# A decode block's tail in four quadrants of 112 columns instead of three of 128 and a doubled 64

## The chip, the cores and the metric

The kernel runs on one core of one Trainium2 chip. The metric is device time in microseconds (us) of one execution; lower is better. Three runs of the kernel before gave 213.26, 213.30 and 213.38 us.

## The reference

One decode step of four tokens (B = 4) of width D = 448: attention over the last W = 1024 cached keys and values, then an MLP, both with a residual.

```python
def _A_ref(x, k_cache, v_cache, wq, wo):      # 16 query heads on 8 key heads, Dh = 256
    q = (x @ wq) ...                          # 448 -> 16 * 256
    scores = jnp.einsum("bhqd,bhkd->bhqk", q, k) * (Dh ** -0.5)
    o = jnp.einsum("bhqk,bhkd->bhqd", _softmax(scores), v)
    return o.reshape(B, Sq, Hq * Dh) @ wo     # 4096 -> 448
def _B_ref(x, w1, b1, w2, b2):
    y = _layernorm(x)
    h = _gelu(jnp.einsum("bsd,df->bsf", y, w1) + b1)   # 448 -> 1792
    return jnp.einsum("bsf,fd->bsd", h, w2) + b2       # 1792 -> 448
h = x + _A_ref(_layernorm(x), k_cache, v_cache, wq, wo)
out = h + _B_ref(_layernorm(h), w1, b1, w2, b2)
```

All of it is in float32. The second part normalizes twice: once outside the MLP and once within it.

## The kernel before, in words

The caches and weights, some 88 MB, are read once, so the kernel is a stream of loads with matmuls between them. All loads are issued on SP's queue in the order of the program (`load`, L58), into three large slots of a ring (`slot`, L51): first the query weights of the first head pair with the tokens `xT` and the biases (`t<-wq`), then keys, then the loads `l1` to `l8`, each a mixture of keys, values, query weights and output weights, then the tail's three slots `te0` to `te2`. The order of PE, SP and ACT is that of the code; DVE and POOL are ordered by the framework.

With four tokens a matmul has only 32 useful output rows. So outputs are laid out in four quadrants of 32 partitions (Q = 32): four matmuls, each with 32 columns of stationary operand, write partitions 0 to 31, 32 to 63, 64 to 95 and 96 to 127, and run side by side.

The tail is what the change touches. Its loads, in the order of the queue, are the last keys `k7`, values with half of an output weight `vo`, the last values `v7` in two pieces, the remaining output weights `wo`, the first MLP weights `w1` in two pieces (L401) and the second MLP weights `w2` in four (L402). Then:

- `add_quadrants` (L265) and `add_rows` (L438) collect the attention output in `ph`: 448 columns cut over the four quadrants by `columns` (L235), 128 to each of the first three, and the last 64 written twice to fill the fourth. A row of the tail is thus a 128 x 128 tile in which quadrant j holds columns 128 j onward of the four tokens.
- `h` (L464) adds the residual and, by `accum_out`, the sum of every row; `row_mean` (L454) turns sums into means with the matrix `fold`, whose last quadrant has half the weight since its columns count twice (L112 to L114). `d` and `z` subtract the means (L469, L474), ACT squares them (L476, L477), and `pz` (L479) transposes `z` to `zT`, 128 rows by four chunks.
- The two normalizations' factors come from POOL (`rsqrt`, L148).
- `pu` (L501) multiplies `zT` by the first MLP weights, 4 chunks by 4 quadrants of 448 columns. Chunks 0 to 2 have 128 rows of weights; the fourth has 64, packed on 128 partitions as two halves of the columns, so its matmuls take 64 rows each (`w1_part`). The order of the chunks is 0, 1, 3, 2, and the first load piece holds 0, 1 and 3.
- `u` (L507, L508) is bias and GELU; `put` and `put_last` (L513, L516) transpose it into `gT` and `gT_last`.
- The second MLP weights have 14 chunks. Chunks 0 to 7 go into `pa` (L528) at full width; ACT copies it to `pas` (L532). Chunks 8 to 13 go into `py` (L539) by quadrants, and after chunk 10 four matmuls with `sel` (L265) add `pas`. `res` (L545) adds the residual and bias `hb`, and is stored (L546).

`keep_warm` matmuls (L269) on an idle tile stand wherever PE would wait.

Of the kernel before, what the change touches and what calls it, by code (L numbers as in the profile page):

```python
# [8 lines left out]
F32 = mybir.dt.float32  # L9
BF16 = mybir.dt.bfloat16  # L10
AF = mybir.ActivationFunctionType
ALU = mybir.AluOpType
# [3 lines left out]
B, D = 4, 448  # L16
# [3 lines left out]
F = 1792  # L20
P = 128
H = P // 2
ND = 4
NKC = W // P
NFC = F // P
FQ = F // 4
Q = 32
CACHE = NKC * B * DH
HALF = CACHE // 2
WEIGHTS = 4 * D  # L30
SLOT = CACHE + 2 * WEIGHTS + HALF
COLUMNS = ND * B + 4 + 4 * 4
EPS = 1e-5
SCALE = DH ** -0.5

# [1 line left out]
def block_kernel(ctx: ExitStack, tc, wq0, k0, wq1, l1, l2, l3, l4, l5, l6, l7, l8, k7, vo, v7, wo, w1, w2, out):  # L37
    nc = tc.nc
    const = ctx.enter_context(tc.tile_pool(name="const", bufs=1))
    ring = ctx.enter_context(tc.tile_pool(name="ring", bufs=3))  # L40
    work = ctx.enter_context(tc.tile_pool(name="work", bufs=2))
    once = ctx.enter_context(tc.tile_pool(name="once", bufs=1))
    ps_s = ctx.enter_context(tc.tile_pool(name="ps_s", bufs=2, space=PSUM))
    ps_t = ctx.enter_context(tc.tile_pool(name="ps_t", bufs=2, space=PSUM))
    ps_o = ctx.enter_context(tc.tile_pool(name="ps_o", bufs=1, space=PSUM))
# [5 lines left out]
    def slot(name):  # L51
        return ring.tile([P, SLOT], F32, tag="r", name=name)

    def load(t, at, src, pieces=None):
        dst = t[:, at : at + src.shape[-1]]
        at = 0
        for n in pieces or (src.shape[-1],):
            nc.sync.dma_start(dst[:, at : at + n], src[:, at : at + n])  # L58
            at += n
        return dst  # L60

    def cut(t, sizes):
        parts, at = [], 0
        for n in sizes:
            parts.append(t[:, at : at + n])
            at += n
        return parts


    def wq_parts(y, t, last=None):  # L70
        parts = [(a, y[:, a, :], slice(0, 512), t[:, a * 512 : (a + 1) * 512]) for a in range(3)]
        if last is not None:
            return parts + [(3, y[:H, 3, :], slice(0, 512), last)]
        for i in range(2):
            parts.append((3, y[:, 3 + i, :], slice(i * 2 * P, (i + 1) * 2 * P), t[:, 3 * 512 :]))
        return parts
# [9 lines left out]
    def output_weights(t):  # L86
        return t.rearrange("p (j e) -> p j e", j=4)
# [9 lines left out]
    sel = const.tile([P, Q], F32, name="sel")  # L97
# [9 lines left out]
    zT = const.tile([P, ND, Q], F32, name="zT")  # L107
# [2 lines left out]

    fold = const.tile([P, 4, Q], F32, name="fold")
    for j in range(4):  # L112
        nc.vector.tensor_scalar_mul(fold[: 3 * Q, j, :], sel[: 3 * Q, :], 1.0 / D)
        nc.vector.tensor_scalar_mul(fold[3 * Q :, j, :], sel[3 * Q :, :], 0.5 / D)  # L114
    fold = fold.rearrange("p j q -> p (j q)")
    rows_of = ident.rearrange("p (j q) -> p j q", j=4)[:, :, :B]
    qT = [const.tile([P, 2, B, Q], F32, name=f"qT{i}") for i in range(2)]
    pT = [const.tile([P, NKC // 2, B, Q], F32, name=f"pT{i}") for i in range(2)]
    oT = [const.tile([P, 4, Q], F32, name=f"oT{i}") for i in range(2)]
    gT = const.tile([P, 12, Q], F32, name="gT")  # L120
    gT_last = const.tile([P, 2, Q], F32, name="gT_last")
    idle = const.tile([P, 512], BF16, name="idle")
    nc.vector.memset(idle, 0.0)
    for t in qT + oT + pT + [gT, gT_last]:
        nc.gpsimd.memset(t, 0.0)

    rs = const.tile([P, 2 * P + FQ], F32, name="rs")
    xb, b2b, b1b = rs[:, :P], rs[:, P : 2 * P], rs[:, 2 * P :]


    def column_mean(t, name):
# [46 lines left out]
    def score_tiles(n):  # L178
        return [ps_s.tile([P, 512], F32, tag="s", name=f"s{n}_{h}") for h in range(2)]
# [53 lines left out]


    def columns(t, j):  # L235
        if j < 3:
            return t[:, j * P : (j + 1) * P].rearrange("p (i c) -> p i c", i=2)
        return t[:, None, 3 * P :].to_broadcast([t.shape[0], 2, H])


    def transposed_output(n, po, rec, groups):
# [35 lines left out]


    t = slot("t0")
    wqt, xT, b2T, b1T = cut(load(t, 0, wq0), (WEIGHTS, ND * B, 4, 4 * 4))  # L280
    wqt = wq_parts(yT[0], wqt)
    xT = xT.rearrange("p (a b) -> p a b", a=ND)
    ka, kb, wqt1 = cut(load(t, WEIGHTS + COLUMNS, k0), (HALF, HALF, 3 * 512))
    for i in range(2):
# [3 lines left out]
    d = work.tile([P, ND, B], F32, tag="d", name="d_x")  # L288
# [10 lines left out]

    wide = t[:, SLOT - 6 * P :].rearrange("p (n j q) -> p n j q", n=6, j=4)  # L300
    nc.vector.tensor_copy(
        wide[:, 0].rearrange("p j (r b) -> p j r b", b=B), xT[:, :, None, :].to_broadcast([P, ND, Q // B, B])
    )
    biases = b1T.rearrange("p (c j) -> p c j", j=4)
    nc.vector.tensor_copy(wide[:, 1], b2T[:, :, None].to_broadcast([P, 4, Q]))
# [10 lines left out]
    s = score_tiles(0)  # L316
# [17 lines left out]
    p, rec = softmax(0, s)  # L334
# [5 lines left out]
    vb, v, wo_a, wo_b = cut(load(slot("l2"), 0, l2), (HALF, CACHE, WEIGHTS, WEIGHTS))  # L340
# [7 lines left out]
    s = score_tiles(1)  # L348
# [5 lines left out]
    k2, v, wq_a, wq_b = cut(load(slot("l4"), 0, l4), (HALF, CACHE, WEIGHTS, WEIGHTS))  # L354
    scores(s, 1, 1, keys(k2))
    p, rec = softmax(1, s)
# [6 lines left out]
    v, wo_a, wo_b, ka = cut(load(slot("l5"), 0, l5), (CACHE, WEIGHTS, WEIGHTS, HALF))  # L363
    values(1, chunks(v), po)
    s = score_tiles(2)
# [8 lines left out]
    p, rec = softmax(2, s)  # L374
# [3 lines left out]
    v, va, wq_a, wq_b = cut(load(slot("l7"), 0, l7), (CACHE, HALF, WEIGHTS, WEIGHTS))  # L378
# [8 lines left out]
    s = score_tiles(3)  # L387
# [5 lines left out]
    e = [slot(f"te{i}") for i in range(3)]  # L393
    kt = [keys(t) for t in cut(load(e[0], 0, k7), (HALF, HALF))]
    v, wot = cut(load(e[1], 0, vo), (CACHE, 2 * D))
# [2 lines left out]
    rest, wo_last = cut(load(e[1], CACHE + 2 * D, wo), (2 * D, WEIGHTS))  # L398
    wot, rest = (t.rearrange("p (j e) -> p j e", j=2) for t in (wot, rest))
    wo_last = output_weights(wo_last)  # L400
    w1t = cut(load(e[0], CACHE, w1, (2 * F + F // 2, F)), (F, F, F // 2, F))  # L401
    w2t = cut(load(e[2], CACHE, w2, (8 * D, 3 * D, 2 * D, D)), NFC * (D,))  # L402
    for h in range(2):
        scores(s, 1, h, kt[h])
    p, rec = softmax(3, s)
# [20 lines left out]

    keep_warm(3, warm)
    values(1, vt_last, po_last, alone=True)
    last = ps_s.tile([P, 512], F32, tag="s", name="last")[:, :P]
    ph = last.rearrange("p (i c) -> p i c", i=2)  # L430
    add_quadrants(ph, accs, True)
    keep_warm(1, warm)
    transposed_output(4, po_last, rec, range(1, 2))
# [9 lines left out]
        add_rows(oT[1], wo_last[:, i, :], i, i == 3)  # L443


    def w1_part(a, j):
        if a < 3:
            return slice(0, P), w1t[3 if a == 2 else a][:, FQ * j : FQ * (j + 1)]
        rows = slice(H * (j // 2), H * (j // 2) + H)
        return rows, w1t[2][rows, FQ * (j % 2) : FQ * (j % 2 + 1)]  # L450


    def row_mean(sums, at, name):
        nc.tensor.matmul(at, fold, sums, start=True, stop=True)  # L454
        return at
# [2 lines left out]
        return once.tile([P, 1], F32, tag=name, name=name)  # L458

    keep_warm(1, warm)  # L460
    h = once.tile([P, P], F32, tag="h", name="h")
    hs, ds = stat("hs"), stat("ds")
    squares = once.tile([P, 2], F32, tag="squares", name="squares")
    nc.vector.scalar_tensor_tensor(h, last, 1.0, xb, op0=ALU.mult, op1=ALU.add, accum_out=hs)  # L464
    pm = ps_m.tile([P, 2], F32, tag="m", name="pm")
    m = row_mean(hs, pm[:, 0:1], "m")
    keep_warm(2, warm)
    d = once.tile([P, P], F32, tag="dh", name="dh")
    nc.vector.tensor_scalar(d, h, m, None, op0=ALU.subtract, op1=ALU.add, accum_out=ds)  # L469
    pm2 = ps_m.tile([P, 2], F32, tag="m", name="pm2")  # L470
    m = row_mean(ds, pm2[:, 0:1], "m2")
    keep_warm(2, warm)
    z = once.tile([P, P], F32, tag="z", name="z")
    nc.vector.tensor_scalar(z, d, m, None, op0=ALU.subtract)  # L474
    junk = once.tile([P, P], F32, tag="junk", name="junk")
    nc.scalar.activation(junk, d, AF.Square, accum_out=squares[:, 0:1])  # L476
    nc.scalar.activation(junk, z, AF.Square, accum_out=squares[:, 1:2])  # L477
    pz = ps_m.tile([P, 4, B], F32, tag="m", name="pz")
    nc.tensor.matmul(pz, z, rows_of, start=True, stop=True)  # L479
    nc.vector.tensor_copy(zT[:, :, :B], pz)  # L480
    hb = once.tile([P, P], F32, tag="hb", name="hb")
    nc.vector.tensor_add(hb, h, b2b)
    keep_warm(2, warm)

# [1 line left out]
    s = stat("r2")  # L486
    u = once.tile([P, FQ], F32, tag="u", name="u")
    pu = ps_s.tile([P, 512], F32, tag="s", name="pu")[:, :FQ]
# [5 lines left out]
    rsqrt(s, v2, "r2")  # L494
    nc.vector.tensor_mul(s, s, r1)
    keep_warm(1, warm)
    for a in (0, 1, 3, 2):
        m = Q if a == 0 else B
        for j in range(4):
            rows, w = w1_part(a, j)  # L500
            nc.tensor.matmul(  # L501
                pu[j * Q : j * Q + m, :], zT[rows, a, :m], w, start=(a == 0), stop=(a == 2),
            )


# [11 lines left out]
    dst = gT.rearrange("p (c j) q -> p c j q", c=3)  # L517
# [6 lines left out]
    first = 8  # L524
    pa = ps_w.tile([P, D], F32, tag="acc", name="pa")
    for c in range(first):
        j, m = c % 4, Q if c < 4 else B
# [2 lines left out]
        )  # L530
    pas = once.tile([P, D], F32, tag="u", name="pas")
    nc.scalar.copy(pas, pa)  # L532
    py = ps_o.tile([P, 2, H], F32, tag="o", name="py")
    for c in range(first, NFC):
        g = gT[:, c, :] if c < 12 else gT_last[:, c - 12, :]
        for j in range(4):
            m, n = (Q, 2) if c == first else (B, 2 if j < 3 else 1)
            w = columns(w2t[c], j) if n == 2 else w2t[c][:, None, 3 * P :]
            nc.tensor.matmul(  # L539
                py[j * Q : j * Q + m, :n, :], g[:, :m], w, start=(c == first), stop=(c == NFC - 1),  # L540
            )
        if c == first + 2:
            add_quadrants(py, pas, False)
    res = once.tile([P, P], F32, tag="res", name="res")
    nc.vector.tensor_add(res, py.rearrange("p i c -> p (i c)"), hb)  # L545
    nc.sync.dma_start(out, res)  # L546


# [76 lines left out]
```

## Time and profile before

| what | value |
|---|---|
| median of three runs | 213.3 us |
| the profiled execution's own time | 213.49 us |
| its span, first to last instruction | 211.7 us |
| bytes read | 88.23 MB |
| granted TensorE clock, mean | 0.878 |
| PE / DVE / ACT busy | 65% / 13% / 7% of the span |

In the profile's rows PE is matmuls, PEld the loading of the stationary operand, DVE, ACT and POOL the vector, scalar and general engines, SPq the issue of loads. A row names output and inputs by tiles (`pu<-te,zT`), the shape as partitions x elements, and a count; a bracket gives the idle time of the engine just before, and what ended it. Float32 matmuls are recorded as two passes each, so 16 matmuls are x32. Times in rows are us from the start of the span.

### The profile page before, as it was taken

The numbers are of one execution on the slowest core, as the hardware profiler recorded it, in microseconds if no ns is written. First come the engines' busy times: TensorE is split into PE (matmuls) and PEld (weight loads), VectorE is DVE, ScalarE is ACT, GpSimd is POOL, SyncE is SP. The second block draws the span as 40 slices with busy tenths as digits, with TensorE's granted clock in tenths as the row PEclk, the third lists the DMA queues.
The fourth block names the chain that finished last, engine by engine and source line by source line (L and its number), as shares of the span: only waits on it lengthen the run. The fifth ranks groups of instructions, "written<-read, shape, count | busy, mean of one in ns | idle before, by whom it ended". The sixth has DMA issues, their size and how long they took to land.

```text
span 211.7 us, 2238 instructions
## 1 busy us (share of the span) xinstructions
PE 137.8 (65%) x976; PEld 47.4 (22%) x976; DVE 27.6 (13%) x135; ACT 14.5 (7%) x34; POOL 5.0 (2%) x17
## 2 busy tenths in 40 slices
PE   0467846802960688198469586639807997888984
PEld 0330202300220232033112122102302222324332
DVE  1510103100020011013002003100100131103210
ACT  2010000200000000021000002000100002010311
POOL 5100000000000000000000000000000000000200
PEclk9999999995899569859959969666975999999999
DMA  7999998999999999999999999999989999999991
GB/s 294 426 397 471 446 489 384 399 517 408 408 396 516 408 411 396 528 396 408 396 446 427 474 408 471 432 420 420 480 350 430 470 433 393 432 399 442 427 400 60
DMA packets 3256, 88.42 MB, mean 418 GB/s; under 512 B 368, under 2 KB 624, under 8 KB 1200
## 3 DMA queue, kind: packets, MB, share of 16 engines
q1 hardware_dynamic: 3248, 88.30, 97.0%
q8 instruction: 7, 0.11, 0.2%
q14 instruction: 1, 0.01, 0.0%
HBM read 88.23 MB, written 0.07 MB: 417 GB/s over the span
## 4 chain that ended last, share of the span: by engine, by line
DMA 80%; PE 15%; SPq 2%; DVE 1%; issue 1%
DMA l<-l 64%; DMA te<-w 16%; PE po L226 8%; PE acc L257 2%; PE s L184 2%; SPq L58 2%; PE pot L247 1%; PE pa L528 1%; SPq L285 1%; PE py L539 1%; DVE o L243 0%; DVE oT L252 0%; DVE oT L253 0%; PE py L265 0%; DVE res L545 0%
## 5 line engine op out<-in xcount | busy, mean ns | idle before, releaser
L226 PE MATMUL po<-l,pT 128*32 128x512 f32 x192 | 29.5, 770 | 26.4 <-DMA l<-l 26.3
L184 PE MATMUL s<-l,qT 128*32 128x512 f32 x192 | 26.3, 692 | 12.4 <-DMA l<-l 11.8
L226 PEld LDWEIGHTS po<-l,pT 128*32 128x32 f32 x192 | 6.9, 135 | 45.6 <-issue 26.5
L184 PEld LDWEIGHTS s<-l,qT 128*32 128x32 f32 x192 | 6.5, 126 | 30.2 <-issue 19.6
L153 PE MATMUL pq<-l,yT 128*32 128x512 f32 (+1 forms) x60 | 8.7, 726 | 6.9 <-DMA l<-l 6.9
L198 ACT ACTIVATE p<-s,nm 128x512 f32<-128x512 f32 x8 | 5.4, 682 | 91.9 <-DVE nm L194 91.9
L269 PE MATMUL between<-idle 128*32 128x512 bf16 x42 | 11.5, 415 | 0.0
L192 DVE TENSOR_REDUCE mx<-s 128x1 f32<-128x512 f32 x8 | 5.5, 692 | 45.7 <-PE s L184 45.7
L243 DVE TENSOR_SCALAR o<-po,rec 128x512 f32<-128x512 f32 x5 | 3.8, 751 | 57.3 <-PE po L226 57.3
L226 PE MATMUL po<-te,pT 128*32 128x512 f32 x64 | 7.3, 595 | 1.3 <-DMA te<-vo 1.2
L269 PEld LDWEIGHTS <-idle 128*32 128x32 bf16 x64 | 5.9, 100 | 9.8 <-issue 6.1
L212 PE MATMUL ppt<-ident,p 128*128 128x128 f32 x32 | 5.0, 283 | 4.2 <-ACT p L198 4.2
L169 DVE TENSOR_REDUCE sm<-pqt 128x32 f32<-128x128 f32 x4 | 1.2, 292 | 46.5 <-PE pqt L167 46.5
L153 PE MATMUL pq<-t,yT 128*32 128x512 f32 (+1 forms) x16 | 3.9, 952 | 4.9 <-DVE yT L295 2.9
L269 PE MATMUL warm<-idle 128*32 128x512 bf16 x22 | 6.6, 382 | 0.0
L153 PEld LDWEIGHTS pq<-l,yT 128*32 128x32 f32 x60 | 3.7, 149 | 12.9 <-DMA l<-l 7.4
L163 ACT COPY qs<-pq 128x512 f32<-128x512 f32 x4 | 2.3, 586 | 60.1 <-PE pq L153 60.1
L257 PE MATMUL acc<-l,oT 128*32 128x448 f32 x48 | 5.1, 545 | 1.4 <-DVE oT L253 1.4
L184 PE MATMUL s<-t,qT 128*32 128x512 f32 x32 | 5.4, 836 | 0.7 <-DVE qT L176 0.7
L148 POOL TENSOR_TENSOR r<-ve_r,mhalf 128x1 f32<-128x1 f32 x2 | 1.1, 544 | 188.8 <-DVE ve_r L147 188.8
L167 PE MATMUL pqt<-ident,qs 128*128 128x128 f32 x16 | 3.5, 360 | 2.9 <-ACT qs L163 2.9
L212 PEld LDWEIGHTS ppt<-ident,p 128*128 128x128 f32 x32 | 3.4, 141 | 7.6 <-ACT p L198 7.6
(117 smaller groups left out, 83.1 us busy)
## 6 DMA issues: line engine op xcount, KB each, us to landing
l<-l SPq DMA_DIRECT2D x6, 7936.0 KB, 46.8
l<-l SPq DMA_DIRECT2D x2, 6144.0 KB, 34.2
t<-k SPq DMA_DIRECT2D x1, 4864.0 KB, 15.8
te<-vo SPq DMA_DIRECT2D x1, 4544.0 KB, 29.4
te<-k SPq DMA_DIRECT2D x1, 4096.0 KB, 40.0
te<-v SPq DMA_DIRECT2D x1, 3072.0 KB, 17.9
te<-w SPq DMA_DIRECT2D x1, 2240.0 KB, 27.5
te<-w SPq DMA_DIRECT2D x1, 1792.0 KB
```

The source lines that it names most:

```text
L58: nc.sync.dma_start(dst[:, at : at + n], src[:, at : at + n])
L153: nc.tensor.matmul(pq[j * Q : (j + 1) * Q, cols], y, w, start=start and cols.start == 0, stop=not start and cols.stop == 512,)
L163: nc.scalar.copy(qs, pq)
L167: nc.tensor.transpose(pt[:, i, :], qs[:, i * P : (i + 1) * P], ident)
L184: nc.tensor.matmul(s[h][b * Q : (b + 1) * Q, :], qT[g][:, c, b, :], kt[:, c, b, :], start=(g == 0 and c == 0), stop=(g == 1 and c == 1),)
L192: nc.vector.reduce_max(mx[:, h : h + 1], s[h], axis=AX.X)
L198: nc.scalar.activation(p[:, h * 512 : (h + 1) * 512], s[h], AF.Exp, bias=nm, scale=SCALE, accum_out=sums[:, h : h + 1],)
L212: nc.tensor.transpose(pt[:, c, :], p[:, (4 * h + c) * P : (4 * h + c + 1) * P], ident)
L226: nc.tensor.matmul(po[b * Q : (b + 1) * Q], pT[g][:, c, b, :], vt[c][:, :, b, :], start=(c == 0 and (alone or g == 0)), stop=(c == NKC // ...
L243: nc.vector.tensor_scalar_mul(o, po, rec)
L257: nc.tensor.matmul(acc[i * Q : (i + 1) * Q, :], oT[g][:, i, :], wt[:, i, :], start=(n == 0 and g == 0), stop=(n == 3 if i < 2 else n == 2 ...
L269: nc.tensor.matmul(warm[:Q], idle[:, :Q], idle, start=True, stop=True)
```

## The change

The tail's rows are cut into four quadrants of R = 112 columns, so that nothing is doubled. `ph`, `h`, `d`, `z`, `hb`, `py` and the sum into `res` become 112 columns wide; `fold` has one weight; `zT` holds 112 rows by four chunks; the first MLP weights lie in four chunks of 112 rows on 112 partitions, the first load piece holding three, the second one. The tokens come a second time in the new cut (`xR`, 16 columns more in the first load), and `res` is cleared on POOL at the start, since its last 16 columns are no longer written. The second MLP weights and all else stay.

```diff
     def load(t, at, src, pieces=None):
-        dst = t[:, at : at + src.shape[-1]]
+        dst = t[: src.shape[0], at : at + src.shape[-1]]
...
     for j in range(4):
-        nc.vector.tensor_scalar_mul(fold[: 3 * Q, j, :], sel[: 3 * Q, :], 1.0 / D)
-        nc.vector.tensor_scalar_mul(fold[3 * Q :, j, :], sel[3 * Q :, :], 0.5 / D)
+        nc.vector.tensor_scalar_mul(fold[:, j, :], sel, 1.0 / D)
...
-    for t in qT + oT + pT + [gT, gT_last]:
+    res = const.tile([P, P], F32, name="res")
+    for t in qT + oT + pT + [gT, gT_last, res]:
         nc.gpsimd.memset(t, 0.0)
...
     def columns(t, j):
-        if j < 3:
-            return t[:, j * P : (j + 1) * P].rearrange("p (i c) -> p i c", i=2)
-        return t[:, None, 3 * P :].to_broadcast([t.shape[0], 2, H])
+        return t[:, j * R : (j + 1) * R]
...
-    w1t = cut(load(e[0], CACHE, w1, (2 * F + F // 2, F)), (F, F, F // 2, F))
+    w1t = cut(load(e[0], CACHE, w1, (3 * F, F)), 4 * (F,))
...
-    h = once.tile([P, P], F32, tag="h", name="h")
+    h = once.tile([P, R], F32, tag="h", name="h")
...
-    nc.tensor.matmul(pz, z, rows_of, start=True, stop=True)
-    nc.vector.tensor_copy(zT[:, :, :B], pz)
+    nc.tensor.matmul(pz[:R], z, rows_of, start=True, stop=True)
+    nc.vector.tensor_copy(zT[:R, :, :B], pz[:R])
...
-    for a in (0, 1, 3, 2):
+    for a in range(ND):
         m = Q if a == 0 else B
         for j in range(4):
-            rows, w = w1_part(a, j)
             nc.tensor.matmul(
-                pu[j * Q : j * Q + m, :], zT[rows, a, :m], w, start=(a == 0), stop=(a == 2),
+                pu[j * Q : j * Q + m, :], zT[:R, a, :m], w1t[a][:R, FQ * j : FQ * (j + 1)],
+                start=(a == 0), stop=(a == ND - 1),
             )
...
-    py = ps_o.tile([P, 2, H], F32, tag="o", name="py")
+    py = ps_o.tile([P, 512], F32, tag="o", name="py")[:, :R]
     for c in range(first, NFC):
         g = gT[:, c, :] if c < 12 else gT_last[:, c - 12, :]
         for j in range(4):
-            m, n = (Q, 2) if c == first else (B, 2 if j < 3 else 1)
-            w = columns(w2t[c], j) if n == 2 else w2t[c][:, None, 3 * P :]
+            m = Q if c == first else B
             nc.tensor.matmul(
-                py[j * Q : j * Q + m, :n, :], g[:, :m], w, start=(c == first), stop=(c == NFC - 1),
+                py[j * Q : j * Q + m], g[:, :m], columns(w2t[c], j), start=(c == first), stop=(c == NFC - 1),
             )
         if c == first + 2:
             add_quadrants(py, pas, False)
-    res = once.tile([P, P], F32, tag="res", name="res")
-    nc.vector.tensor_add(res, py.rearrange("p i c -> p (i c)"), hb)
+    nc.vector.tensor_add(res[:, :R], py, hb)
...
-    w1 = packed(np.asarray(B_w1))
-    w1 = np.concatenate([w1[:, : 2 * F], w1[:, 3 * F :], w1[:, 2 * F : 3 * F]], axis=1)
+    w1 = np.asarray(B_w1).reshape(4, R, F).transpose(1, 0, 2).reshape(R, 4 * F)
```

The order of no engine changes in the tail; the shapes do. On SP, the loads of the last output weights (`wo`), of the first MLP weights (the two rows into the same tile `te` behind it) and of the second (the four behind) stood so before:

```order
L58 DMA te_697<-wo 128x2688
L58 DMA te_696<-w 128x4480
L58 DMA te_696<-w 128x1792
L58 DMA te_698<-w 128x3584
L58 DMA te_698<-w 128x1344
```

and stand so now:

```order
L59 DMA te_695<-wo 128x2688
L59 DMA te_694<-w 112x5376
L59 DMA te_694<-w 112x1792
L59 DMA te_696<-w 128x3584
L59 DMA te_696<-w 128x1344
```

The first MLP weights have 112 rows where they had 128; the rows of the first piece are longer, and nothing moves in the queue. On PE, at the kernel's end, the chunks 8 to 13 of the second MLP weights into `py`, with the four `sel` matmuls on `pas` among them, were

```order
L539 MATMUL py<-te_698,gT 32x128 x4
L539 MATMUL py<-te_698,gT 4x128 x3
L539 MATMUL py<-te_698,gT 4x64
L539 MATMUL py<-te_698,gT 4x128 x3
L539 MATMUL py<-te_698,gT 4x64
L265 MATMUL py<-pas,sel 32x128 x4
L539 MATMUL py<-te_698,gT 4x128 x3
L539 MATMUL py<-te_698,gT 4x64
L539 MATMUL py<-te_698,gT_last 4x128 x3
L539 MATMUL py<-te_698,gT_last 4x64
```

and are now

```order
L520 MATMUL pa<-te_696,gT 4x448 x4
L530 MATMUL py<-te_696,gT 32x112 x4
L530 MATMUL py<-te_696,gT 4x112 x8
L264 MATMUL py<-pas,sel 32x112 x4
L530 MATMUL py<-te_696,gT 4x112 x4
L530 MATMUL py<-te_696,gT_last 4x112 x8
```

As many matmuls stand in the same order, all 112 wide, where each group of four had three of 128 and one of 64.

More of the change, by code (lines that the diff above doesn't have):

```diff
@@ L31 @@
 SLOT = CACHE + 2 * WEIGHTS + HALF
-COLUMNS = ND * B + 4 + 4 * 4
+R = D // 4
+COLUMNS = 2 * ND * B + 4 + 4 * 4
 EPS = 1e-5
@@ L123, in block_kernel @@
     nc.vector.memset(idle, 0.0)
-    for t in qT + oT + pT + [gT, gT_last]:
+    res = const.tile([P, P], F32, name="res")
+    for t in qT + oT + pT + [gT, gT_last, res]:
         nc.gpsimd.memset(t, 0.0)
     rs = const.tile([P, 2 * P + FQ], F32, name="rs")
-    xb, b2b, b1b = rs[:, :P], rs[:, P : 2 * P], rs[:, 2 * P :]
+    xb, b2b, b1b = rs[:, :R], rs[:, P : P + R], rs[:, 2 * P :]
     def column_mean(t, name):
@@ L279, in block_kernel @@
     t = slot("t0")
-    wqt, xT, b2T, b1T = cut(load(t, 0, wq0), (WEIGHTS, ND * B, 4, 4 * 4))
+    wqt, xT, xR, b2T, b1T = cut(load(t, 0, wq0), (WEIGHTS, ND * B, ND * B, 4, 4 * 4))
     wqt = wq_parts(yT[0], wqt)
@@ L301, in block_kernel @@
     nc.vector.tensor_copy(
-        wide[:, 0].rearrange("p j (r b) -> p j r b", b=B), xT[:, :, None, :].to_broadcast([P, ND, Q // B, B])
+        wide[:, 0].rearrange("p j (r b) -> p j r b", b=B),
+        xR.rearrange("p (a b) -> p a b", a=ND)[:, :, None, :].to_broadcast([P, ND, Q // B, B]),
     )
@@ L428, in block_kernel @@
     values(1, vt_last, po_last, alone=True)
-    last = ps_s.tile([P, 512], F32, tag="s", name="last")[:, :P]
-    ph = last.rearrange("p (i c) -> p i c", i=2)
+    ph = ps_s.tile([P, 512], F32, tag="s", name="ph")[:, :R]
     add_quadrants(ph, accs, True)
@@ L443, in block_kernel @@
         add_rows(oT[1], wo_last[:, i, :], i, i == 3)
[L446 to L450, printed above, removed]
     def row_mean(sums, at, name):
@@ L460, in block_kernel @@
     keep_warm(1, warm)
-    h = once.tile([P, P], F32, tag="h", name="h")
+    h = once.tile([P, R], F32, tag="h", name="h")
     hs, ds = stat("hs"), stat("ds")
     squares = once.tile([P, 2], F32, tag="squares", name="squares")
-    nc.vector.scalar_tensor_tensor(h, last, 1.0, xb, op0=ALU.mult, op1=ALU.add, accum_out=hs)
+    nc.vector.scalar_tensor_tensor(h, ph, 1.0, xb, op0=ALU.mult, op1=ALU.add, accum_out=hs)
     pm = ps_m.tile([P, 2], F32, tag="m", name="pm")
@@ L467, in block_kernel @@
     keep_warm(2, warm)
-    d = once.tile([P, P], F32, tag="dh", name="dh")
+    d = once.tile([P, R], F32, tag="dh", name="dh")
     nc.vector.tensor_scalar(d, h, m, None, op0=ALU.subtract, op1=ALU.add, accum_out=ds)
@@ L472, in block_kernel @@
     keep_warm(2, warm)
-    z = once.tile([P, P], F32, tag="z", name="z")
+    z = once.tile([P, R], F32, tag="z", name="z")
     nc.vector.tensor_scalar(z, d, m, None, op0=ALU.subtract)
-    junk = once.tile([P, P], F32, tag="junk", name="junk")
+    junk = once.tile([P, R], F32, tag="junk", name="junk")
     nc.scalar.activation(junk, d, AF.Square, accum_out=squares[:, 0:1])
@@ L478, in block_kernel @@
     pz = ps_m.tile([P, 4, B], F32, tag="m", name="pz")
-    nc.tensor.matmul(pz, z, rows_of, start=True, stop=True)
-    nc.vector.tensor_copy(zT[:, :, :B], pz)
-    hb = once.tile([P, P], F32, tag="hb", name="hb")
+    nc.tensor.matmul(pz[:R], z, rows_of, start=True, stop=True)
+    nc.vector.tensor_copy(zT[:R, :, :B], pz[:R])
+    hb = once.tile([P, R], F32, tag="hb", name="hb")
     nc.vector.tensor_add(hb, h, b2b)
@@ L602 @@
     w2 = w2.transpose(1, 0, 2).reshape(P, NFC * D)
-    b2 = np.asarray(B_b2)
-    b2 = np.concatenate([b2, b2[3 * P :]]).reshape(ND, P).T
+    xR = np.zeros((P, ND * B), np.float32)
+    xR[:R] = x.reshape(B, 4, R).transpose(2, 1, 0).reshape(R, 4 * B)
+    b2 = np.zeros((P, 4), np.float32)
+    b2[:R] = np.asarray(B_b2).reshape(4, R).T
     b1 = np.zeros((4, 4 * P), np.float32)
@@ L609 @@
     arrays = {
-        "wq0": np.concatenate([wq[0], xT, b2, b1], axis=1), "k0": k0, "wq1": wq1, **loads, "k7": k[7], "vo": vo, "v7": v[7], "wo": wo_end, "w1": w1, "w2": w2,
+        "wq0": np.concatenate([wq[0], xT, xR, b2, b1], axis=1), "k0": k0, "wq1": wq1, **loads, "k7": k[7], "vo": vo, "v7": v[7], "wo": wo_end, "w1": w1, "w2": w2,
     }
@@ L623 @@
     got = np.asarray(r.results[0]["out"]).reshape(4, Q, P)[:, :B, :]
-    return np.ascontiguousarray(got.transpose(1, 0, 2).reshape(B, 1, 4 * P)[:, :, :D])
+    return np.ascontiguousarray(got[:, :, :R].transpose(1, 0, 2).reshape(B, 1, D))
```

## The prediction

> **What bounds the kernel now.** I read the page's totals first, then the stretches of time, the timeline of the last 20 us and the chain. The page, its DMA share in 40 slices, the bytes, and the chain by engine:
>
> ```profile
> span 211.7 us, 2238 instructions
> PE 137.8 (65%) x976; PEld 47.4 (22%) x976; DVE 27.6 (13%) x135; ACT 14.5 (7%) x34; POOL 5.0 (2%) x17
> DMA  7999998999999999999999999999989999999991
> HBM read 88.23 MB, written 0.07 MB: 417 GB/s over the span
> DMA 80%; PE 15%; SPq 2%; DVE 1%; issue 1%
> ```
>
> No engine is busy for two thirds of the span; the 16 DMA engines are, in every slice but the first and the last. The stretches (duration, busy time of PE, PEld, DVE, ACT and POOL, then clock, DMA share, GB/s) show it as a rate:
>
> ```profile
> 20.00:60.00 40.00, 22.75 (x151) 7.18 (x150) 4.38 (x22) 2.04 (x5) 0.00 (x0) 0.91 1.03 443
> 60.00:120.00 60.00, 39.30 (x260) 13.12 (x260) 5.62 (x31) 2.62 (x6) 0.00 (x0) 0.80 0.99 428
> 120.00:170.00 50.00, 32.43 (x214) 9.62 (x218) 4.67 (x23) 2.03 (x5) 0.00 (x0) 0.80 1.00 433
> 190.00:201.00 11.00, 10.00 (x118) 4.60 (x110) 3.26 (x14) 2.09 (x5) 1.09 (x2) 1.00 1.01 433
> 201.00:205.00 4.00, 3.72 (x29) 1.65 (x25) 1.02 (x3) 1.01 (x4) 0.00 (x0) 1.00 0.95 398
> 205.00:209.00 4.00, 3.56 (x73) 1.67 (x72) 0.00 (x0) 0.53 (x1) 0.00 (x0) 1.00 0.51 204
> ```
>
> From 20 to 205 us the loads run at 398 to 443 GB/s with a share of about 1: there is no spare rate in which a load that loses time could catch up. So whatever delays a load near the end delays all behind it. The sizes at the end of the queue, and the waits in the timeline (start, duration, what, and in brackets the idle time before and what ended it):
>
> ```profile
> te<-w SPq DMA_DIRECT2D x1, 2240.0 KB, 27.5
> te<-w SPq DMA_DIRECT2D x1, 896.0 KB
> te<-w SPq DMA_DIRECT2D x1, 1792.0 KB
> ```
>
> ```profile
> 193.31 1.25 PEld L438 LDWEIGHTS last<-te,oT 128*32 128x32 f32 x48 [0.42 <-DMA te<-wo]
> 193.32 1.52 PE L438 MATMUL last<-te,oT 128*32 128x128 f32 x48
> 198.71 3.44 PE L501 MATMUL pu<-te,zT 128*32 128x448 f32 x32 [0.19 <-DMA te<-w]
> 201.21 0.11 PEld L501 LDWEIGHTS pu<-te,zT 128*4 128x4 f32 x8 [0.75 <-DMA te<-w]
> 202.29 0.81 DVE L507 SCALAR_TENSOR_TENSOR u<-pu,r,rs 128x256 f32<-128x256 f32 x2 [1.95 <-PE pu L501]
> 204.42 0.34 ACT L521 COPY gT_last<-put_last 64x8 f32<-64x8 f32 x2 [0.93 <-PE put_last L516]
> 205.43 1.71 PE L528 MATMUL pa<-te,gT 128*32 128x448 f32 x16 [0.34 <-DMA te<-w]
> 206.94 0.56 PEld L539 LDWEIGHTS py<-te,gT 128*32 128x32 f32 x24 [0.63 <-DMA te<-w]
> 207.25 0.53 ACT L532 COPY pas<-pa 128x448 f32<-128x448 f32 x1 [2.48 <-PE pa L528]
> 207.84 0.43 PE L265 MATMUL py<-pas,sel 128*32 128x128 f32 x8
> 208.21 0.73 PE L539 MATMUL py<-te,gT_last 128*4 128x64 f32 x16
> 209.02 0.29 DVE L545 TENSOR_TENSOR res<-py,hb 128x128 f32<-128x128 f32 x1 [4.66 <-PE py L539]
> ```
>
> PE stops for one load after another: the last output weights (193.31), the first MLP weights in two pieces (198.71 and 201.21), then the second MLP weights (205.43, 206.94). From 205.43 on the chain is work: pa, the copy pas, four sel matmuls, the last chunks, the sum res. The MLP's own chain is ready earlier: gT_last ends at 204.42 + 0.34 = 204.76, 0.67 us before its weights.
>
> **The change, part by part.** *Tail matmuls and vector work.* Before 205.43 nothing of this is on the path. The 48 passes of L438 cover 128 columns instead of 112; the ops on h, d, z and hb shrink alike; whatever they save only lengthens the wait for the first MLP weights at 198.71. Behind 205.43 lie four groups of four matmuls side by side (sel, and the chunks 11 to 13), two passes each. What a pass costs by width is in the tile view of py (min/median/max ns):
>
> ```profile
> L539 PE MATMUL py<-te,gT_last x16: 219/272/273, 208.2 to 208.7; 128*4 128x128 f32 x12, 128*4 128x64 f32 x4
> ```
>
> and an op of DVE on 16 columns stands in the timeline:
>
> ```profile
> 193.13 0.17 DVE L253 TENSOR_TENSOR oT<-oT,pot 128x16 f32<-128x16 f32 x1
> ```
>
> A 64-wide pass takes 219 ns and a 128-wide one 272, so 0.83 ns a column; a group ends with its widest matmul, so 16 columns fewer give 13 ns a pass and 4 × 2 × 13 = 0.11 us. The sum res costs 0.29 us at 128 columns against 0.17 for such an op at 16: 1.07 ns a column, so 0.02 us less. Together −0.13 us; the ends are 0 (PE is still fed by landings there) and an eighth of 0.43 + 0.73 + 0.29 and a little for chunk 11, some −0.25.
>
> *Start.* Four DVE ops fewer for fold, 0.18 us each; one memset more on POOL, of which two cost 0.35; 8 KB more in the first load.
>
> ```profile
> 9.96 0.18 DVE L114 TENSOR_SCALAR fold<-sel 32x32 f32<-32x32 f32 x1
> 1.72 0.35 POOL L125 MEMSET oT<- 128x128 f32 x2
> 9.27 1.03 POOL L148 TENSOR_TENSOR rx<-ve_x,mhalf 128x4 f32<-128x4 f32 x1 [5.81 <-DVE sel L98]
> 17.05 1.93 PE L153 MATMUL pq<-t,yT 128*32 128x512 f32 x6 [2.01 <-DMA t<-k]
> ```
>
> The memset lies in POOL's 5.81 us of idle time; the DVE time comes off ahead of the first projection, behind which PE waits 2.01 us for the keys anyway. Both cost and bring nothing; without that cover the memset would cost 0.18 us. The 8 KB cost 0.02 us at 430 GB/s, on the queue that bounds the kernel.
>
> *The first MLP weights.* 2240 + 896 = 3136 KB become 112 × 5376 × 4 B = 2352 KB and 112 × 1792 × 4 B = 784 KB: the same 3136 KB. The first piece grows by 112 KB, 0.27 us at 430 GB/s, so the matmuls of L501, which stand back to back from 198.71, start 0.27 later; that comes out of the 0.67 us ahead of 205.43. Two row groups of 64 go, and the 16 matmuls keep their 448 columns: nothing. What is left is whether 112 rows load as fast as 128. This load now takes 201.21 − 193.31 = 7.90 us from landing to landing. All other large loads of the trace have 128 rows, eight for each of 16 engines; the only load without is this one:
>
> ```profile
> wq_last<-wq SPq DMA_DIRECT2D x2, 64.0 KB
> ```
>
> It has 32 rows twice and 64 KB, too little to read a rate from. So no row prices the load, and I bound it: at the one end +0, if seven longer rows an engine take what eight shorter ones did; at the other each row shares its way into SBUF with a second engine's all the time, at half the rate: +7.90 us. [...] I take the middle, half of the load at half the rate: **+4.0 us**, and keep both ends. An unequal load also ends unevenly, and engines that are done go on with the second weights, so some of the loss comes back; the middle stands for that too.
>
> [...]
>
> Sum: 211.7 − 0.13 + 0.02 + 4.0 = 215.6 us of span. The profiled execution took 213.49 us, 1.79 more than its span, and the median of the three runs is 213.3, 0.19 less: 215.6 + 1.79 − 0.19 = **217.2 us**.
>
> **The rivals.** *The load stays even* (the other side: not slower). Seven rows of 28,672 B in all are as many bytes for an engine as eight of 25,088; if engines alone set the rate, the tail's −0.11 is all that happens: 213.2 us. For it: the same bytes, 16 engines, a share of 1.0 whatever the row's length. Against it: no load of the trace has tried it. It decides as long as no two engines meet for longer than 0.5 us in total.
>
> *Only the used partitions count.* If groups of eight partitions each take in at a fixed rate, and no engine is held up otherwise, a full group gets 8 rows of 28,672 B instead of 25,088, a seventh more: 7.90 / 7 = +1.1 us, 214.3 us. This is the mild form of my forecast: it would need engines to fill gaps without waiting. [...]
>
> *A pile-up.* If the engines' rows fall in step so that four at a time share a way, the load takes four times as long: 3 × 7.90 = +23.7 us, 236.9. Against it: engines that start and end at different times drift out of step.
>
> *Faster.* Without any cost the load's 7.90 us may shrink: 3.21 MB at the 433 GB/s of its stretch are 7.42 us. With fewer, longer rows closing that gap: −0.48 − 0.11, so 212.7 us. Against it: the row count an engine falls only from 16 to 14, and nothing in the trace ties the gap to the number of rows.
>
> **How the numbers follow.** A measurement of this kernel can tell about 0.2%, 0.43 us, from no change. Forecast (2 to 7.9 us more) 0.42; even load 0.33; only the used partitions 0.14; pile-up 0.06; faster 0.05. Slower by over 0.2%: 0.42 + 0.14 + 0.06 = 0.62; within 0.2%: 0.33; faster: 0.05. The forecast alone spans 215.2 to 221.1. The range must also hold the even load, so it begins at 213.0, the tail's larger saving included; it leaves out the pile-up, the faster case and the top of the forecast's span, and ends at 220.0.
>
> **What would show it.** In the changed profile PE's wait for the second piece of the first MLP weights, now ended at 201.21, ends 4 us later, and so does the start of pa, now at 205.43; the GB/s in the stretch from 193 to that landing fall to some 270 (3.21 MB in 11.9 us). The tail behind pa's start keeps its length but for some 0.1 us. The span up to 190 us is unchanged within 0.3 us. If pa starts within 0.4 us of 205.43, the forecast's step on the load is wrong and the even load right; if 1 us later, the seventh. If pa waits for gT_last and not for DMA, the first weights came so late against the second that the MLP's chain became the bound.

## The result and the profile after

The changed kernel takes 221.95 us (median of five runs, 221.62 to 222.58) against 213.30 (213.16 to 213.38): a ratio of 1.041, 95% interval 1.039 to 1.044, or 8.65 us more. The forecast was 217.2 us with a range of 213.0 to 220.0. All medians, ranges and intervals below leave out one slow execution, 225.31 us of e4_warm, which lies more than 1.5% above the fastest of its kernel. The profiled execution of the changed kernel has a span of 220.2 us, 8.5 more than before. Its page:

```profile
span 220.2 us, 2235 instructions
PE 140.4 (64%) x976; PEld 48.3 (22%) x976; DVE 26.4 (12%) x131; ACT 14.5 (7%) x34; POOL 5.1 (2%) x18
DMA  7989999899899899989999999999999999999980
GB/s 285 452 374 435 438 467 522 369 404 519 369 404 509 384 392 508 404 381 499 439 429 460 392 407 484 404 404 484 403 396 466 436 393 397 429 225 251 300 338 16
HBM read 88.24 MB, written 0.07 MB: 401 GB/s over the span
```

The DMA engines look as busy as before to the end, but slices 36 to 38 of the 40 (some 193 to 209 us) move 225, 251 and 300 GB/s: here a busy share of 0.9 and more says that packets are under way, not that they move at the 419 GB/s of the kernel before. Two stretches of the kernel before (columns as in the prediction: the clock, the DMA share and the GB/s stand last):

```profile
170.00:190.00 20.00, 17.44 (x119) 5.47 (x111) 3.71 (x16) 1.98 (x5) 0.00 (x0) 1.00 0.99 423
195.00:203.00 8.00, 7.57 (x52) 2.67 (x51) 2.78 (x13) 2.28 (x6) 1.09 (x2) 1.00 0.98 419
```

and of the changed kernel:

```profile
170.00:190.00 20.00, 17.58 (x115) 5.49 (x111) 3.70 (x16) 1.98 (x5) 0.00 (x0) 1.00 0.99 423
195.00:203.00 8.00, 4.79 (x64) 2.77 (x64) 2.10 (x11) 2.06 (x5) 1.08 (x2) 1.00 0.96 238
203.00:205.00 2.00, 0.00 (x0) 0.00 (x0) 0.00 (x0) 0.00 (x0) 0.00 (x0) 0.67 1.09 262
205.00:207.00 2.00, 1.35 (x8) 0.41 (x12) 0.00 (x0) 0.00 (x0) 0.00 (x0) 0.50 1.05 258
207.00:209.00 2.00, 2.00 (x16) 0.53 (x12) 0.00 (x0) 0.00 (x0) 0.00 (x0) 0.50 0.93 355
211.00:213.00 2.00, 1.72 (x14) 0.91 (x9) 0.81 (x2) 0.69 (x2) 0.00 (x0) 1.00 0.98 394
```

Up to 190 us the kernels are alike. With the first MLP weights the rate falls to 238 GB/s, where the kernel before has 419, and comes back when they are in (394 GB/s from 211 to 213 us). PE does nothing from 203 to 205 us, and its granted clock falls to 0.50. The timeline of the changed kernel, at the steps that were shown of before:

```profile
195.10 1.36 PE L437 MATMUL ph<-te,oT 128*32 128x112 f32 x48 [1.74 <-DMA te<-wo]
205.65 5.60 PE L492 MATMUL pu<-te,zT 112*32 112x448 f32 x32 [5.56 <-DMA te<-w]
211.39 0.81 DVE L499 SCALAR_TENSOR_TENSOR u<-pu,r,rs 128x256 f32<-128x256 f32 x2 [9.48 <-PE pu L492]
213.53 0.34 ACT L513 COPY gT_last<-put_last 64x8 f32<-64x8 f32 x2 [0.93 <-PE put_last L508]
214.00 1.31 PE L520 MATMUL pa<-te,gT 128*32 128x448 f32 x12
216.42 0.40 PE L264 MATMUL py<-pas,sel 128*32 128x112 f32 x8 [0.15 <-ACT pas L524]
216.83 0.57 PE L530 MATMUL py<-te,gT_last 128*4 128x112 f32 x16
217.46 0.28 DVE L535 TENSOR_TENSOR res<-py,hb 128x112 f32<-128x112 f32 x1 [4.00 <-PE py L530]
```

`pu` starts 205.65 − 198.71 = 6.94 us later: the load. The matmuls of L437 were late already, 195.10 for 193.32: the last packets of the output weights, which have 128 rows as before, run beside the first of the slow load and take up to 815 ns, where they took 404. `pu` takes 5.60 us instead of 3.44, 2.16 more: the clock. From the start of `u` to the start of `res` pass 6.07 us instead of 6.73, 0.66 less, since `pa` no longer waits for its weights. 6.94 + 2.16 − 0.66 = 8.44 us, the whole difference in the start of `res` (217.46 against 209.02). The chain of the changed kernel says the same in order of time: a landing at 205.52, and from there only work (its main pieces).

```profile
170.85 34.67 DMA te<-w
205.52 0.14 issue
205.65 5.64 PE pu L492 x32
211.39 0.49 DVE u L499
211.91 0.43 ACT u L500
212.37 0.84 PE put L505 x6
214.19 1.57 PE pa L520 x11
```

### The profile page after: what moved, and what is told of

Its sections match the earlier page's. It is cut to its first block, busy times and chain, and to the rows that moved or that the text cites. A ratio compares the mean times of both kernels' runs of the same rounds, so it can differ in the third digit from the quotient of the medians.

```text
span 220.2 us, 2235 instructions
## 1 busy us (share of the span) xinstructions
PE 140.4 (64%) x976; PEld 48.3 (22%) x976; DVE 26.4 (12%) x131; ACT 14.5 (7%) x34; POOL 5.1 (2%) x18
## 4 chain that ended last, share of the span: by engine, by line
DMA 77%; PE 18%; SPq 2%; DVE 1%; issue 1%; ACT 0%; DVEq 0%; ACTq 0%
DMA l<-l 61%; DMA te<-w 16%; PE po L227 7%; PE pu L492 3%; PE acc L256 2%; PE s L185 2%; SPq L59 1%; PE pot L246 1%; PE pa L520 1%; SPq L284 1%; PE put L505 0%; DVE o L242 0%; PE py L530 0%; DVE oT L251 0%; PE warm L268 0%
## 5 line engine op out<-in xcount | busy, mean ns | idle before, releaser
L227 PE MATMUL po<-l,pT 128*32 128x512 f32 x192 | 30.5, 792 | 24.6 <-DMA l<-l 24.5
L185 PE MATMUL s<-l,qT 128*32 128x512 f32 x192 | 28.3, 739 | 14.0 <-DMA l<-l 13.4
L185 PEld LDWEIGHTS s<-l,qT 128*32 128x32 f32 x192 | 7.1, 131 | 32.6 <-issue 20.8
L154 PE MATMUL pq<-l,yT 128*32 128x512 f32 (+1 forms) x60 | 8.2, 690 | 5.9 <-DMA l<-l 5.9
L268 PE MATMUL between<-idle 128*32 128x512 bf16 x42 | 10.2, 379 | 0.0
L492 PE MATMUL pu<-te,zT 112*4 112x448 f32 (+1 forms) x32 | 5.6, 874 | 5.6 <-DMA te<-w 5.6
```

Source lines behind the costliest of these rows:

```text
L154: nc.tensor.matmul(pq[j * Q : (j + 1) * Q, cols], y, w, start=start and cols.start == 0, stop=not start and cols.stop == 512,)
L185: nc.tensor.matmul(s[h][b * Q : (b + 1) * Q, :], qT[g][:, c, b, :], kt[:, c, b, :], start=(g == 0 and c == 0), stop=(g == 1 and c == 1),)
L227: nc.tensor.matmul(po[b * Q : (b + 1) * Q], pT[g][:, c, b, :], vt[c][:, :, b, :], start=(c == 0 and (alone or g == 0)), stop=(c == NKC // ...
L268: nc.tensor.matmul(warm[:Q], idle[:, :Q], idle, start=True, stop=True)
L492: nc.tensor.matmul(pu[j * Q : j * Q + m, :], zT[:R, a, :m], w1t[a][:R, FQ * j : FQ * (j + 1)], start=(a == 0), stop=(a == ND - 1),)
```

## The experiments

| kernel | what it is | median us | beside the kernel before | ratio, 95% interval |
|---|---|---|---|---|
| e1_pad128 | changed, weights padded to 128 rows | 215.42 | 213.34 | 1.007 to 1.011 |
| e2_bytes | before, as many bytes as e1 | 215.49 | 213.34 | 1.006 to 1.011 |
| e3_halves64 | before, load in 64 + 64 partitions | 223.12 | 213.34 | 1.044 to 1.047 |
| e4_warm | changed, PE kept at work | 221.69 | 213.34 | 1.034 to 1.042 |
| e5_pitch | changed, other row distance in HBM | 221.03 | 213.33 | 1.032 to 1.041 |
| e6_eights | before, rows in 16 blocks of eight | 221.41 | 213.33 | 1.037 to 1.040 |
| e7_pad128_warm | e1, PE kept at work | 214.37 | 213.33 | 1.004 to 1.006 |
| e8_bytes_warm | e2, PE kept at work | 214.34 | 213.33 | 1.004 to 1.006 |
| e9_quarters32 | before, load in 4 x 32 partitions | 222.86 | 213.41 | 1.043 to 1.046 |
| e10_eighths16 | before, load in 8 x 16 partitions | 227.83 | 213.41 | 1.061 to 1.071 |

**Is it the 112 rows or the tail?** e1_pad128 undoes the 112 rows alone:

```diff
     w1 = np.asarray(B_w1).reshape(4, R, F).transpose(1, 0, 2).reshape(R, 4 * F)
+    w1 = np.concatenate([w1, np.zeros((P - R, 4 * F), np.float32)], axis=0)
```

> The changed kernel with the first MLP weights padded by 16 rows of zeros to 128 rows on 128 partitions (3584 KB instead of 3136 KB); all else of the change stays. Theory 'shared ways' (16 equal shares of seven rows make engines write into the same group of partitions at once): with eight rows an engine the load runs at the usual 433 GB/s again, so the time is 213.3 + 1.06 us for 459 KB more, less 0.13 for the narrower tail: 214.2 us. Rival 'the tail' (narrow matmuls and new layout cost the time, or PE's clock by itself): the time stays near 222 us.

It took 215.42 us, in two groups: 214.36 and 214.59, and four runs from 215.42 to 215.89. So some 6.5 us of the 8.65 go by 16 rows of zeros more. Its rate in the stretch is as high as in the kernel before:

```profile
195.00:203.00 8.00, 6.48 (x49) 2.77 (x50) 1.83 (x11) 2.06 (x5) 1.08 (x2) 1.00 1.00 427
```

The single DMA packets of the two traces say the same. One row of the first piece is a packet of 21,504 B in both kernels. In e1_pad128 all 128 of them take 799 ns; in the changed kernel the 112 take 908 to 1989 ns, 1357 in the median. Not one row came at the old speed.

e2_bytes gives the old tail as many bytes:

```diff
-    w1t = cut(load(e[0], CACHE, w1, (2 * F + F // 2, F)), (F, F, F // 2, F))
+    w1t = cut(load(e[0], CACHE, w1, (3 * F, F)), (F, F, F // 2, F // 2, F))
+    w1t = w1t[:3] + w1t[4:]
...
-    w1 = np.concatenate([w1[:, : 2 * F], w1[:, 3 * F :], w1[:, 2 * F : 3 * F]], axis=1)
+    w1 = np.concatenate([w1[:, : 2 * F], w1[:, 3 * F :], np.zeros((P, F // 2), np.float32), w1[:, 2 * F : 3 * F]], axis=1)
```

> The kernel before with its first MLP weights made as large as those of e1_pad128, by 896 unused columns on all 128 partitions (3584 KB). Bytes alone: 213.3 + 1.06 = 214.4 us under every theory. Against e1_pad128 it leaves only the tail's width: 0.13 us more than e1_pad128 by the sum of the prediction, no difference if PE is fed by landings to the end, less than e1_pad128 if the narrow tail costs.

215.49 us, again in two groups (214.27 and 214.28; 215.34 to 215.71). The tail's 0.13 us can't be seen through that. The profile of e2_bytes, from the upper group, shows what parts them; the stretch and the timeline:

```profile
199.00:205.00 6.00, 5.35 (x35) 1.20 (x36) 0.84 (x4) 0.00 (x0) 0.54 (x1) 0.72 1.01 427
```

```profile
199.65 4.89 PE L502 MATMUL pu<-te,zT 128*32 128x448 f32 x32 [1.25 <-DMA te<-w]
```

The load runs at 427 GB/s, but the clock has a mean of 0.72 from 199 to 205 us (0.92 from 195 to 200 and 0.74 from 200 to 205: as an estimate from these means, 0.50 from some 199.2 to 202.6) and `pu` takes 4.89 us. e7_pad128_warm and e8_bytes_warm keep PE at work through that wait, the same edit on e1 and on e2:

```diff
     nc.vector.tensor_mul(s, s, r1)
-    keep_warm(1, warm)
+    keep_warm(7, warm)
```

> e1_pad128 with 7 instead of 1 matmul on the idle tile ahead of pu. Runs of e1_pad128 lay at 214.4 to 214.6 and at 215.4 to 215.9 us. Theory 'PE's clock halves in some runs during the longer wait ahead of pu': with PE at work through the wait only the lower group is left, 214.3 us. Rival 'the landings themselves differ': both groups stay. Against e8_bytes_warm: 0.13 us less for the narrower tail.

> e2_bytes with 7 instead of 1 matmul on the idle tile ahead of pu. Theory 'clock': only the lower group of its runs is left, 214.4 us, where e2_bytes had 214.3 and 215.3 to 215.7. Rival: both groups stay.

Both lose the upper group: 214.25 to 214.52 and 214.27 to 214.57 us. In e8_bytes_warm `pu` takes 3.44 us again, and `pa` starts at 206.35:

```profile
199.85 3.44 PE L502 MATMUL pu<-te,zT 128*32 128x448 f32 x32
206.35 1.71 PE L529 MATMUL pa<-te,gT 128*32 128x448 f32 x16
```

So the clock can cost 1.0 us (between the medians of e1's groups) to 1.4 us (of e2's) in this tail, behind a wait of 1.25 us in the profiled run of e2_bytes. The 448 KB more (459 thousand bytes) cost 214.34 − 213.33 = 1.0 us, for 1.06 expected. And the medians of the two, 214.37 and 214.34, show nothing of the narrower tail's 0.13 us. With 128 rows the changed tail is as fast as the old one, so the loss is that of the load of 112 rows and of what its delay brings.

**Is it the way into SBUF?** e3_halves64 leaves the old kernel as it is, and loads each piece of the same weights in two halves of the partitions:

```diff
-    w1t = cut(load(e[0], CACHE, w1, (2 * F + F // 2, F)), (F, F, F // 2, F))
+    w1d, at = e[0][:, CACHE : CACHE + 3 * F + F // 2], 0
+    for n in (2 * F + F // 2, F):
+        for rows in (slice(0, H), slice(H, P)):
+            nc.sync.dma_start(w1d[rows, at : at + n], w1[rows, at : at + n])
+        at += n
+    w1t = cut(w1d, (F, F, F // 2, F))
```

> The kernel before, with each of its two pieces of the first MLP weights loaded in two: partitions 0 to 63, then 64 to 127. Bytes, row lengths, layout and compute unchanged. Theory 'shared ways': 16 engines write into 64 partitions, so two share a way all the time; the load takes twice as long, some 7.4 us more, and PE grows cold while it waits: 220 to 223 us. Rival 'only the used partitions count' or 'the odd number of seven rows': all 128 partitions are used and an engine has four rows of each half, so 213.3 to 213.7 us.

223.12 us, 0.1 above the upper end of what the theory gave, and far from the rival. Half the rate, and PE waits (5.18 us) and its clock falls to 0.50 (from 205 to 209 us) as in the changed kernel; the stretch and the timeline of e3_halves64:

```profile
195.00:203.00 8.00, 4.96 (x64) 2.92 (x64) 2.16 (x11) 2.09 (x5) 1.08 (x2) 1.00 1.01 219
```

```profile
205.37 4.82 PE L506 MATMUL pu<-te,zT 128*32 128x448 f32 x24 [5.18 <-DMA te<-w]
214.48 1.71 PE L533 MATMUL pa<-te,gT 128*32 128x448 f32 x16 [0.23 <-DMA te<-w]
```

`pa` starts 9.05 us later than before, more than the 7.4 us of a load of twice the time; where the rest comes from isn't settled. All 128 partitions are filled and no row is longer, so "only the used partitions count" falls. What the edit changes is how many partitions a load writes: with 64 at a time instead of 128 the stretch runs at 219 GB/s instead of 419. e6_eights goes a step further and writes all 128 in each load, the rows only stored in blocks:

```diff
+    w1 = np.concatenate([w1.reshape(16, 8, -1), np.zeros((16, 1, 3 * F + F // 2), np.float32)], axis=1)
...
+        nc.sync.dma_start(w1d[:, at : at + n], w1[:, :8, at : at + n])
```

> The kernel before, with the first MLP weights stored as 16 blocks of eight rows (and an unused ninth row a block, so that the blocks don't merge). 128 rows on 128 partitions, bytes, layout and compute as before. [...] Rival 'the number of partitions': 128 are written, so 213.3 us. 213.3 would also come if the rows are dealt out to the engines as before in spite of the blocks; the rate of the stretch tells whether they are.

221.41 us: the load of 128 rows is as slow as that of 112.

```profile
195.00:203.00 8.00, 6.37 (x64) 3.84 (x64) 2.00 (x10) 2.09 (x5) 1.08 (x2) 0.80 0.97 215
```

So it is neither the number of partitions nor the odd seven, and since there are two loads, as in the kernel before, it isn't the number of loads either. Why these loads are slow isn't shown: the profile has no row for one DMA engine, so which rows and partitions an engine takes, and whether two engines share a way into SBUF, stay assumptions of the author. The blocks also change how far apart in HBM the rows lie that are read at once; this run alone doesn't rule that out.

e5_pitch turns to the other end, the distance between rows in HBM:

```diff
+    w1 = np.concatenate([w1, np.zeros((R, 1024), np.float32)], axis=1)
...
-    w1t = cut(load(e[0], CACHE, w1, (3 * F, F)), 4 * (F,))
+    w1t = cut(load(e[0], CACHE, w1[:, : 4 * F], (3 * F, F)), 4 * (F,))
```

> The changed kernel with the rows of the first MLP weights 4 KB further apart in HBM (1024 unused columns behind each row, not loaded). Theory 'shared ways into SBUF': where the rows are read from does not matter, 221.6 to 222.6 us as the changed kernel. Rival 'the source' (the distance of the rows that the 16 engines read at once makes them collide in HBM): the load changes its rate, and the time moves by more than 1 us either way, to about 214 us if the collisions go.

221.03 us, with single runs from 219.69 to 222.66. The low rate stays: no run is near 214, and from 195 to 200 and from 200 to 205 us the load runs at 268 and 222 GB/s, where the changed kernel has 267 and 219. The scatter is wider than the first expectation allowed, so a difference of 1 us from the source can't be excluded.

**How many partitions at a time?** e9_quarters32 and e10_eighths16 cut the load of e3_halves64 finer:

```diff
-        for rows in (slice(0, H), slice(H, P)):
+        for r in range(0, P, 32):              # 16 in e10_eighths16
+            rows = slice(r, r + 32)
```

> e3_halves64 with the same pieces loaded in four: 32 partitions at a time. [...] Theory B, a way is eight neighbouring partitions: 32 reach four ways, the load takes four times its 7.4 us, some 22 us more than before, 234 to 238 us. [...]

> The same with 16 partitions at a time. [...] Theory B: two ways, up to eight times, up to 52 us more. Rival 'any load on fewer than 128 partitions costs the same': 223 us as e3_halves64.

222.86 us for 32 partitions at a time: no more than for 64 (223.12); theory B is out by 11 us. For 16 at a time 227.83, above the rival's 223 and far below what B gave. The stretches of e9_quarters32 and of e10_eighths16:

```profile
195.00:203.00 8.00, 6.70 (x62) 3.43 (x62) 1.42 (x7) 2.09 (x5) 0.00 (x0) 0.65 0.96 202
```

```profile
195.00:203.00 8.00, 6.27 (x64) 3.94 (x64) 1.57 (x8) 2.07 (x5) 0.12 (x1) 0.79 1.00 143
```

219, 202 and 143 GB/s for 64, 32 and 16 partitions at a time: 32 are nearly as fast as 64, and 16 clearly slower. Why the loss comes in these steps, no run shows. The packets go the same way: a row of the first piece, 17,920 B, takes 667 ns in the kernel before, and in the median 1351, 1374 and 1987 ns with 64, 32 and 16 partitions at a time (1354 in e6_eights).

**How much is the clock in the changed kernel?** e4_warm fills its wait:

```diff
     nc.vector.tensor_mul(s, s, r1)
-    keep_warm(1, warm)
+    keep_warm(24, warm)
```

> The changed kernel with 24 instead of 1 matmul on the idle tile ahead of pu, so that PE works through the wait for the first MLP weights. Theory 'the cold clock is part of the cost': pu runs at full clock in 3.4 us instead of 5.6, and the end falls back on the landing of the second MLP weights at about 212.4 us, 1.3 us less in all: 220.6 us. Rival 'the load is all': pa waits for its weights as late as before, 221.9 us.

221.69 us, with runs from 220.19 to 223.08: the median is 0.3 us lower, within the scatter, and the lowest run is 1.4 us below the lowest of the changed kernel. By their spans from the first to the last instruction, the runs lie at 218.4 to 219.9 us against 219.8 to 220.8 of the changed kernel, 0.7 less in the median, about half of what was expected. In the profile of e4_warm `pu` keeps its clock (1.00 from 203 to 209 us) and `pa` waits for DMA again, as expected, but the load itself landed later, at 213.45 and not at some 212.4:

```profile
206.75 2.45 PE L492 MATMUL pu<-te,zT 112*32 112x448 f32 x21
213.58 1.71 PE L520 MATMUL pa<-te,gT 128*32 128x448 f32 x16 [0.28 <-DMA te<-w]
```

The runs of e4_warm lie up to 2.9 us apart, so what the clock adds to the changed kernel's median is not settled. For the profiled run of the changed kernel it can be estimated. The last of the second MLP weights land at 215.79 us, 7.3 later than before (208.50), and where PE waits for this landing, `res` starts about 0.5 us behind it (209.02 before). By the loads alone `res` would have started at some 216.3; it started at 217.46, so the clock's part is some 1.2 us.

## Why the prediction was wrong, point by point

- **What bounds the kernel** was right: a load that loses time near the end delays all behind it. The rate before and behind the first MLP weights is the old one, and nothing was caught up: the last of the second MLP weights land 7.3 us later than before, about as late as the first weights.
- **The first MLP weights, +4.0 us**: that the load of 112 rows loses rate was right, the size was wrong. "I take the middle, half of the load at half the rate" is the step that failed. The last packet of this load ends at 207.70 us and not at 200.35, 7.35 later and not 4.0, close to the upper end of +7.90, which stood for every row at half the rate. The stretch ran at 238 GB/s where the prediction had some 270, and no packet ran at the old speed: in the mean they took 1.70 times as long in the first piece (1358 ns for 799) and 1.79 times in the second (487 for 272), where half of the load at half the rate would make it 1.5 times. e3_halves64 and e6_eights show the upper end reached: 219 and 215 GB/s, half of 433.
- **What the middle rested on**: no run shows the half of the load at half the rate that the +4.0 us stand for, nor a way into SBUF that two engines share, nor the seven or eight rows an engine, which are 112 and 128 divided by 16; the middle was the author's choice between two bounds. In its place the runs showed every row of the 112 slow (908 ns at the least in the first piece, for 799 in e1_pad128), and 128 rows just as slow when they are stored in blocks of eight (215 GB/s in e6_eights, 238 in the changed kernel). So the number of rows alone doesn't part the fast load from the slow one.
- **What follows from a longer wait** was missing. The prediction priced the delay as a shift of all that comes after, at unchanged durations. PE waited 5.56 us, its clock fell to 0.50, `pu` took 2.16 us more, and the MLP's chain became the bound: `pa` followed `put`, `put_last` and the `warm` matmuls behind them, and no longer a landing. The prediction named such a turn as a sign to look for (with `gT_last`, which `pa` doesn't read) and gave it no price, and it had no term for the clock, although its profile had rows with a clock of 0.80. Of the 2.16 us, some 1.2 reached the end in the profiled run, by the estimate above.
- **The range** ended at 220.0, 1.1 us below the top of the forecast's own span of 215.2 to 221.1. The loads alone, 7.3 us, would have given some 220.6, past the range and within that span; with the clock the result passed that top too, by 0.85 us.
- **The tail, −0.13 us**: its size was about right, but where the loads come in time it is worth nothing. From the start of the `sel` matmuls to that of `res` the changed kernel takes 217.46 − 216.42 = 1.04 us. The same steps at the old width take 1.15 in e2_bytes, where the weights also lay ready:

```profile
209.71 0.43 PE L265 MATMUL py<-pas,sel 128*32 128x128 f32 x8
210.86 0.29 DVE L546 TENSOR_TENSOR res<-py,hb 128x128 f32<-128x128 f32 x1 [4.11 <-PE py L540]
```

  In e7_pad128_warm and e8_bytes_warm it is 3.55 and 3.59 us from the start of `pa` to the start of `res` (206.21 to 209.76; 206.35 to 209.94), only 0.04 less, and the medians show no difference.

```profile
206.21 1.75 PE pa L520 x16
208.03 0.54 ACT pas L524
208.61 0.40 PE py L264 x8
209.01 0.73 PE py L530 x24
209.76 0.28 DVE res L535
```

  The chain of e7_pad128_warm looks like work alone. But the last of the second weights land at 209.28 there and at 209.43 in e8_bytes_warm, and the last chunk's matmuls start at 209.32 and 209.47, right behind them. PE is fed by landings to the end: the case that the prediction named as the upper end, 0. In the kernel before it is the same, with the last landing at 208.50, so the prediction's "From 205.43 on the chain is work" was not quite right.
- **The start** cost nothing, as forecast: 170 to 190 us have the same rate, and `po` and `pot` of the last head run at the same times within 0.3 us.
- **The rivals**: the even load (213.2 us), only the used partitions (214.3) and faster (212.7) are excluded by the result, and the first two as general rules by e3_halves64 and e6_eights. The pile-up in its full form, +23.7 us, didn't come: even 16 partitions at a time gave 14.4 us more. The direction was right, and slower had the larger chance, 0.62.

None of these versions is faster than the kernel before: the narrower tail needs either the 112-row load or 1.0 us of padding, and brings nothing that can be measured.

## What to carry to other kernels

Where loads bound a kernel, do not price a load by its bytes alone; look at how many partitions it writes at one time and at how its rows are stored. Here the same 3.2 MB cost 8 to 10 us of kernel time more in each of four shapes that spread them otherwise (112 rows 8.65, halves 9.78, quarters 9.45, and 128 rows in blocks 8.08 us). A busy share near 1.0 with a falling GB/s is how such a load looked in the profile (0.96 at 238 GB/s). And the wait that grew ahead of the matmuls was not only a shift (5.56 us, with the clock at 0.50 behind it): look whether PE's clock holds through such a wait.

## What the runs showed of the hardware that was not expected

- A load of 128 rows on 128 partitions fell to 215 GB/s from 419 by the way its rows were stored in HBM (16 blocks of eight). What in it makes the load slow is not shown.
- PE's clock halved (to 0.50) in the profiled run of e2_bytes within a wait of only 1.25 us (by the estimate above, some 0.8 us into it), and stayed at 1.00 in that of e1_pad128 behind 1.45 us; the runs of both lie 1.0 to 1.4 us apart in two groups, and six matmuls more on an idle tile left one group. In the changed kernel it fell to 0.50 within a wait of 5.56 us. What sets the moment of the fall, these runs don't show.
- Two kernels with the slow load of 112 rows scatter: 219.69 to 222.66 us for e5_pitch and 220.19 to 223.08 for e4_warm, where the changed kernel stays within 1.0 us and the kernel before within 0.7 us.
